# Attention with routed experts on one core: the products with V two key tiles at a time, behind every second block of scores

## The chip, the core and the metric

The kernel runs on one core of a Trainium2 chip. The engines of that core run side by side, each through its own queue in order: TensorE (PE; its weight loads are listed apart as PEld), VectorE (DVE), ScalarE (ACT), GpSimd (POOL) and SyncE (SP), which here issues nearly all transfers. They wait for each other by semaphores. The metric is the time of one execution in microseconds (us) on the device.

## The reference

Three stages, one behind the other. The change lies in the first.

```python
def _attn_ref(q, k, v, centroids):          # q, k, v: 2 x 8 x 768 x 64
    ...
    q_assign = np.argmax(np.einsum('bhsd,hcd->bhsc', q_n, c_n), axis=-1)
    k_assign = np.argmax(np.einsum('bhsd,hcd->bhsc', k_n, c_n), axis=-1)
    mask = q_assign[:, :, :, None] == k_assign[:, :, None, :]
    scores = scale * np.matmul(q, k.transpose(0, 1, 3, 2))
    scores = np.where(mask, scores, -1000000000.0)
    scores = scores - np.max(scores, axis=-1, keepdims=True)
    attn = np.exp(scores)
    attn = attn / (np.sum(attn, axis=-1, keepdims=True) + 1e-09)
    return np.matmul(attn, v)
```

Behind it every token goes to one of 8 experts (two products with a ReLU between, weighted by the gate's probability), and a last stage multiplies a projection of the tokens with the sigmoid of a causal convolution over them and projects once more.

## The kernel before

The attention goes through 8 groups `g`, each one batch and two heads (768 queries, 768 keys, 64 dimensions). A group has two units `u` of 384 queries, 16 units in all. A unit has 6 blocks `j`: three query tiles `t` of 128 rows by two heads `h`. The main loop (L748) runs over the 96 blocks `i`; "block 8" below means `i % 12 == 8`, that is a place in the group, unless a unit is named.

What one block issues, in this order:

- `do_S(i + 2)`: the scores of the block after next, 128 queries by 768 keys, in a PSUM tile `s` (pool `ps_s`, two slots). Two products of L607 and two of L611, the latter with 80 rows that hold the rest of the split and the mask. VectorE takes the row maximum `mx` (L618).
- `do_T(i)`: six transposes of the probabilities `pexp` (L642), three for each half of the keys, into PSUM tiles `tp` of 3 x 128 columns (pool `ps_t`, two slots, so one for each half). A copy carries each half to `pt` in SBUF: the second half by ScalarE (L647), the first by VectorE (L645) in blocks 0, 1, 7, 8, 10 and 11, and by ScalarE in the others and all through the last unit.
- `do_exp(i + 2)`: ScalarE's exponential with the row sum (L627), from `s` to `pexp`.
- `do_PV(u - 1, j)`: for key tile `j` of the unit before, the products of V with the transposed probabilities (L654): two, one for each head. The stationary tile is 128 keys x 64 dimensions, so head 0 fills the rows 0 to 63 of `pv` in PSUM and head 1 the rows 64 to 127; the six key tiles of a unit are summed there. `pv` has one slot. Behind key tile 5 ScalarE copies it to `ut` (`post1`, L663).
- The preparation of the next group, one list per block: in block 0 the products `dott` (L349, a stationary tile 32 wide) and ScalarE's L331, in block 1 `dots` (L359) and L334, in blocks 2 and 4 the choice of the cluster on VectorE (and GpSimd), in block 5 the transposes `pr` (L388) and ScalarE's `ohr` (L398), and SyncE's transfers of the stacked operands `st` in blocks 3 and 5.
- `post2(u - 2)`: in block 3 of a unit (in groups 4 and 5 in block 4 of a unit) the products `po` (L679), which turn `ut` back to rows of tokens and form the router's logits.

In the last unit (`u == 15`) the products with V of unit 14 are issued three key tiles at a time in its first two blocks, and its own go query tile by query tile (`last_PV`). In the first unit there are none. In groups 4 and 5 the blocks 6 to 9 also carry the routing of the first batch, small operations on VectorE for the most part.

A schedule written out by hand sets the order on every engine: each engine runs its instructions as the code issues them. `tc.manual_schedule()` leaves that order alone and adds the waits. A product that writes to a PSUM slot waits until the copy that read the slot before is through.

Of the kernel before, what the change touches and what calls it, by code (L numbers as in the profile page):

```python
# [16 lines left out]
DRAM = bass.MemoryType.DRAM  # L17
# [15 lines left out]
def routed_attention_moe_kernel(  # L33
# [65 lines left out]
    nc.scalar.activation(warm[:, 1:2], warm[:, 0:1], AF.Sqrt)  # L99

    def keep_warm(ps, n):
        """Products that nothing reads, so that the array's clock is up when the data arrive."""
        for _ in range(n):
            nc.tensor.matmul(ps, onesb, onesb.unsqueeze(1).to_broadcast([128, 4, 128]), start=True, stop=True)

# [38 lines left out]
    nc.scalar.dma_start(cw64, convw.bitcast(I32).rearrange("p (f w) -> p f w", w=2))  # L144

    def fill_slots():
        """Every place of a row starts as zeros that belong to no token; one piece per call."""
        padrow = wstg.tile([128, XC], F32, tag="w", name="padrow")
        nc.gpsimd.memset(padrow, 0.0)
        nc.gpsimd.memset(padrow[:, 513:514], PADID)  # L150
        for d, n in ((xslots, E * CAP // 128), (xover, NCH)):
            dv = d.rearrange("(r p) c -> p r c", p=128)
            for r in range(0, n, 2):
                yield nc.sync.dma_start(
                    dv[:, r:r + 2], padrow.rearrange("p (o c) -> p o c", o=1).to_broadcast([128, 2, XC])
                )
# [2 lines left out]
    cs = cst.tile([128, 6, 4], F32, name="cs")  # L159

    def cent_norm():
        """One over each centroid's norm: the square root once more by Newton's step."""
        v = nc.vector
        v.tensor_tensor(csq, cent_sb, cent_sb, op=ALU.mult)
        v.tensor_reduce(cs[:, 0], csq, axis=AX.X, op=ALU.add)
        nc.scalar.activation(cs[:, 1], cs[:, 0], AF.Sqrt)
        v.tensor_scalar(cs[:, 1], cs[:, 1], 1e-30, None, op0=ALU.max)
        v.reciprocal(cs[:, 2], cs[:, 1])
        v.tensor_tensor(cs[:, 2], cs[:, 2], cs[:, 0], op=ALU.mult)
        v.tensor_tensor(cs[:, 3], cs[:, 1], cs[:, 2], op=ALU.add)  # L170
        v.tensor_scalar(cs[:, 4], cs[:, 3], 0.5, 1e-6, op0=ALU.mult, op1=ALU.add)
        v.reciprocal(cs[:, 5], cs[:, 4])
# [8 lines left out]
    nc.vector.memset(cumb[:, 0, :], 0.0)  # L181
    nc.vector.tensor_copy(xnat[:, :, 513], tokid)

# [1 line left out]
    worder = []  # L185
    for e in range(E + 1):
        worder += [(e, 0), (e, 1)]
# [5 lines left out]
    wld = dram.tile([2, 128, 2048], F32, name="wld")  # L193

    def double_bits(w, t1, t2, top):
        """Of doubles w: the 29 last bits t1, sign and exponent t2, and the float32 just below in size, top."""
        lo, hi = w[:, :, 0], w[:, :, 1]
        v = nc.vector
        return [
            lambda: v.tensor_scalar(t1, hi, 3, 0x3FFFFFF8, op0=ALU.logical_shift_left, op1=ALU.bitwise_and),  # L200
            lambda: v.scalar_tensor_tensor(t1, hi, -0x40000000, t1, op0=ALU.bitwise_and, op1=ALU.bitwise_or),
            lambda: v.scalar_tensor_tensor(t1, lo, 29, t1, op0=ALU.logical_shift_right, op1=ALU.bitwise_or),
            lambda: v.tensor_scalar(t2, hi, 0x7FF00000, None, op0=ALU.bitwise_and),
            lambda: v.scalar_tensor_tensor(
                top, t2, float(897 << 20), t1.bitcast(F32), op0=ALU.is_ge, op1=ALU.mult
            ),
            lambda: v.tensor_scalar(t1, lo, 0x1FFFFFFF, None, op0=ALU.bitwise_and),
            lambda: v.tensor_scalar(t2, top.bitcast(I32), -0x00800000, None, op0=ALU.bitwise_and),
        ]

    def convert_steps(ws):
        """The output stage's doubles, as a rounded float32 and its rest, to DRAM: one entry per step."""
        steps = []
        wi = ws.rearrange("p a b -> p (a b)")
        raw = [wi[:, 1024 * r:1024 * r + 1024] for r in range(2)]
# [61 lines left out]
    ovf = {}  # L277

    def raw(j):
        """The overflow's first weights stay whole: float32 products suit its few columns better."""  # L280
        return worder[j] in ((E, 0), (E, 1))

    def w_dma(j):
# [34 lines left out]
        nc.scalar.copy(hi[:, c], t[:, c])  # L318
        (lo_eng or nc.vector).tensor_tensor(lo[:, c], t[:, c], hi[:, c].bitcast(F32), op=ALU.subtract)  # L319

# [1 line left out]
    def prep_steps(g):  # L322
        b, p = pairs[g]
        x = X[g]
# [86 lines left out]
            nc.sync.dma_start(st[h][64:80, 3, :].bitcast(F32), r[16 * h:16 * h + 16, :])  # L411

        def S0(h, parts=None):
            """The first scores, from the parts where they lie; the mask when it is there."""
            if parts:
                S_[h] = ps_s.tile([128, 2, 512], F32, tag="s", name="s")
                r = slice(64 * h, 64 * h + 64)
# [156 lines left out]
    scattered = {}  # L574

    def scatter(dst, idx, src, n, why=None):
        """Rows to dst at idx, those at n or beyond left out; no two rows of a dst share a place."""
        ins = nc.gpsimd.indirect_dma_start(
            out=dst[:, :],
            out_offset=bass.IndirectOffsetOnAxis(ap=idx, axis=0),  # L580
# [112 lines left out]
    last = {}  # L693

    def last_PV(t):
        """The last unit goes tile by tile, so that little of it is left behind the last scores."""
        g = items[6 * UL][0]
        if t == 0:
            PVs[UL] = ps_v.tile([128, 384], F32, tag="pv", name="pv")
# [48 lines left out]
    for i in range(NI):  # L748
# [9 lines left out]
        if u == U - 1:  # L758
# [2 lines left out]
                    do_PV(u - 1, 3 * j + kt)  # L761
            if j == 1:
                post1(u - 1)
        elif u:
            do_PV(u - 1, j)
            if j == 5:
                post1(u - 1)
        if i % 12 < len(prep):
# [45 lines left out]

    keep_warm(ps_t.tile([128, 512], F32, tag="t", name="spin3"), 34)

# [1 line left out]
    tot = small.tile([128, E], F32, tag="tot", name="tot")  # L818
    nc.vector.tensor_copy(tot, carry["tot"])
    cmp_ = small.tile([128, E, NCH], F32, tag="cmp", name="cmp")  # L820
# [27 lines left out]
    nc.vector.tensor_copy(idx1, osl)  # L848
    aps.close()

# [1 line left out]
    xs_p = mpool("xs", 2)  # L852
    xt_p = mpool("xt", 2)
    h_p = mpool("hp", 2)
# [157 lines left out]

    keep_warm(ps_h.tile([128, 512], F32, tag="h", name="spin"), 20)

# [1 line left out]
    nch = nc.values_load(infoi[0:1, 0:1], min_val=0, max_val=NCH)  # L1016
    with tc.For_i(1, nch, 1) as j:
        ej = nc.sync.value_load(infoi[0:1, bass.ds(j + 1, 1)], min_val=0, max_val=E - 1)
        if True:
# [29 lines left out]
            y = y_p.tile([128, 512], F32, tag="y", name="yl")  # L1049
            nc.scalar.activation(y, yp, AF.Copy, scale=xs[:, 0, 512:513])  # L1050
            scatter(x2d, ids[:, 0:1], y, 2 * S)
# [1 line left out]
    mps.close()  # L1053
    moe.close()
    fin = ExitStack()
# [189 lines left out]
```

## Time and profile before

| | |
|---|---|
| median of 3 runs | 593.78 us (593.48 to 594.0) |
| span of the profiled execution | 598.3 us |
| TensorE busy | 566.0 us, 95% |
| weight loads (PEld) | 438.5 us, 73% |
| VectorE | 391.5 us, 65% |
| ScalarE | 334.5 us, 56% |
| GpSimd | 156.0 us, 26% |

A line of a timeline gives the start from the span's start, the length, the engine, the source line and the operation with the tiles that it writes and reads; "x2" merges equal instructions in a row, and a bracket gives the idle time of that engine before and what ended it. The ends of TensorE's products are modelled and overlap the next start, so the distance between two starts is the measure there. A float32 product appears as two records, so the two products of one key tile with V are "x4". The attention takes the span up to some 275 us, the experts up to some 480, the last stage the rest.

### The profile page before, as it was taken

The page shows a single profiled execution, that of the slowest core. Times are in us where ns is not written, and L with a number is a line of the kernel's source. Part 1 is how long each engine was busy: PE and PEld are TensorE (multiplying, and loading weights), DVE is VectorE, ACT ScalarE, POOL GpSimd, SP SyncE. Part 2 cuts the span into 40 slices and gives each one's busy share as a digit, 9 for nine tenths or more (in the row PEclk, how much of TensorE's full clock was granted, in tenths as well). Part 3 has the DMA queues.
Part 4 walks back from the last instruction along what each step waited for, and adds up shares of the span by engine and source line. Part 5 has one row for each costly group of instructions (what it writes and reads, how often), then busy time and mean ns, then how long its engine had stood idle before and what let it go on. Part 6 is the DMA issues. An engine that isn't in the chain of part 4 may idle for free. (4 is left out here: it accounts for less than half of the span.)

```text
span 598.3 us, 9364 instructions
## 1 busy us (share of the span) xinstructions
PE 566.0 (95%) x3474; PEld 438.5 (73%) x3474; DVE 391.5 (65%) x644; ACT 334.5 (56%) x603; POOL 156.0 (26%) x121
## 2 busy tenths in 40 slices
PE   8599999999999999997889999999999998887997
PEld 3376666666766666674689989989889884776886
DVE  6375666566787875557358688687677480799940
ACT  3387767686767677763146555637555352363432
POOL 3101010010121110113450504406235333555320
PEclk8699999999999999998889999999999998998999
DMA  6967776664564737021637688685786865600112
GB/s 146 258 136 231 163 230 148 210 129 124 113 192 83 204 78 210 1 72 65 244 115 272 220 286 275 218 295 200 264 309 222 356 260 203 263 1 1 54 72 88
DMA packets 33103, 104.82 MB, mean 175 GB/s; under 512 B 5713, under 2 KB 6225, under 8 KB 27936
## 3 DMA queue, kind: packets, MB, share of 16 engines
q1 hardware_dynamic: 29104, 97.84, 53.0%
q0 software_dynamic: 3280, 6.32, 2.8%
q8 instruction: 28, 0.46, 0.3%
q10 hardware_dynamic: 672, 0.06, 0.1%
q14 instruction: 19, 0.16, 0.1%
HBM read 63.45 MB, written 24.95 MB: 148 GB/s over the span
## 5 line engine op out<-in xcount | busy, mean ns | idle before, releaser
L618 DVE TENSOR_REDUCE mx<-s 128x1 f32<-128x768 f32 x96 | 91.7, 956 | 66.9 <-PE s L611 62.7
L319 DVE TENSOR_TENSOR wlo<-wraw,whi 128x1024 fp32r<-128x1024 f32 x66 | 85.5, 1297 | 33.9 <-ACT whi L318 33.3
L647 ACT COPY pt<-tp 128x384 f32<-128x384 f32 x148 | 65.8, 482 | 68.9 <-PE tp L642 66.6
L318 ACT CAST whi<-wraw 128x1024 fp32r<-128x1024 f32 x68 | 70.1, 1044 | 42.5 <-DMA wraw<-in_wq_dram 39.5
L627 ACT ACTIVATE pexp<-s,mx 128x768 f32<-128x768 f32 x96 | 87.0, 906 | 3.1 <-DVE mx L618 2.6
L642 PE MATMUL tp<-ident,pexp 128*128 128x128 f32 x576 | 79.6, 274 | 0.0
L654 PE MATMUL pv<-pt,vt 128*64 128x384 f32 x360 | 77.1, 510 | 0.0
L642 PEld LDWEIGHTS tp<-ident,pexp 128*128 128x128 f32 x576 | 69.2, 141 | 4.2 <-ACT pt L647 0.5
L607 PE MATMUL s<-st 128*128 128x384 f32 x188 | 58.1, 390 | 1.7 <-ACT pexp L627 1.7
L607 PEld LDWEIGHTS s<-st 128*128 128x128 f32 x188 | 28.5, 190 | 37.1 <-ACT pt L647 22.7
L976 PE MATMUL yp<-whi,hhi 128*128 128x512 f32 x136 | 53.8, 396 | 0.0
L979 PE MATMUL yp<-wlo,hhi 128*128 128x512 f32 x136 | 53.7, 395 | 0.0
L980 PE MATMUL yp<-whi,hlo 128*128 128x512 f32 x136 | 53.7, 395 | 0.0
L1113 DVE SCALAR_TENSOR_TENSOR gt<-xf,convw_sb,gt 128x768 f32<-128x768 f32 x32 | 52.2, 1648 | 1.7 <-ACT gt L1109 1.1
L611 PE MATMUL s<-st 80*128 80x384 f32 x188 | 49.0, 342 | 0.0
L337 POOL TENSOR_TENSOR xx<-xkq,xx 128x768 fp32r<-128x768 f32 x8 | 14.5, 1815 | 123.9 <-DVE dsb L354 71.7
L236 POOL TENSOR_TENSOR wspace<-wspace 128x512 f32<-128x512 f32 x8 | 14.3, 1784 | 117.8 <-ACT wspace L232 106.8
L949 PE MATMUL hps<-xhi,whi 128*128 128x256 f32 x256 | 42.9, 288 | 1.4 <-ACT xhi L923 0.7
L953 ACT ACTIVATE hhi<-hps 128x512 fp32r<-128x512 f32 (+1 forms) x36 | 20.7, 575 | 41.1 <-PE hps L949 32.9
L949 PE MATMUL hps<-xhi,wlo 128*128 128x256 f32 x256 | 42.1, 287 | 1.0 <-issue 1.0
L949 PE MATMUL hps<-xlo,whi 128*128 128x256 f32 x256 | 41.4, 284 | 0.0
L954 DVE SCALAR_TENSOR_TENSOR hlo<-hps,hhi 128x512 fp32r<-128x512 f32 (+1 forms) x36 | 23.7, 658 | 24.0 <-issue 15.7
(218 smaller groups left out, 983.1 us busy)
## 6 DMA issues: line engine op xcount, KB each, us to landing
wraw<-in_wq_dram SPq DMA_DIRECT2D x34, 1024.0 KB, 5.5
st<-xx SPq DMA_DIRECT2D x48, 384.0 KB, 6.9
xkq<-in_kq_dram SPq DMA_DIRECT2D x16, 384.0 KB, 4.4
xslots<-padrow SPq DMA_DIRECT2D x8, 514.0 KB, 7.8
wspace<-in_wd_dram SPq DMA_DIRECT2D x8, 512.0 KB, 5.4
xs<-xslots SPq DMA_DIRECT2D x7, 514.0 KB
vt<-in_v_dram SPq DMA_DIRECT2D x8, 384.0 KB, 4.9
out_dram<-os SPq DMA_DIRECT2D x11, 256.0 KB, 2.0
```

Source lines behind the costliest of these rows:

```text
L318: nc.scalar.copy(hi[:, c], t[:, c])
L319: (lo_eng or nc.vector).tensor_tensor(lo[:, c], t[:, c], hi[:, c].bitcast(F32), op=ALU.subtract)
L607: nc.tensor.matmul(ps[:, n, :384], st[:, 1, q0:q0 + 128], st[:, 0, 384 * n:384 * n + 384], start=True, stop=False)
L618: nc.vector.tensor_reduce(mx, ps[:, :, :384], axis=AX.XY, op=ALU.max, negate=True)
L627: nc.scalar.activation(pt, ps[:, :, :384], AF.Exp, bias=mx[:, 0:1], accum_out=Zt[i // 6][:, t, h:h + 1])
L642: nc.tensor.transpose(tp[:, k, :], p[:, 128 * kt:128 * kt + 128], ident)
L647: nc.scalar.copy(dst, tp)
L654: nc.tensor.matmul(PVs[u][64 * h:64 * h + 64, :], Vt[g][:, kt, h, :], PT[u, h][:, kt, :], start=(kt == 0), stop=(kt == NQT - 1), skip_grou ...
L949: nc.tensor.matmul(hp[:, fi, :w], a[:, d, fs], c[:, d, :w], start=(n + d == 0), stop=(n + d == 5))
L976: nc.tensor.matmul(yp[t], hhi[:, fa, ts], whv[:, f, :], start=(q == 0 and f == 0), stop=False)
L979: nc.tensor.matmul(yp[t], hhi[:, fa, ts], wlv[:, f, :], start=False, stop=False)
L980: nc.tensor.matmul(yp[t], hlo[:, fa, ts], whv[:, f, :], start=False, stop=(q == 1 and f == 3))
```

## The change

In units 1 to 14 an even block issues no product with V any more, and an odd one issues those of two key tiles, its own and that of the block before: j = 0 and 1 behind block 1 of the unit, 2 and 3 behind block 3, 4 and 5 behind block 5. The first and the last unit stay as they are. The diff also drops comments and docstrings, which changes no instruction.

```diff
--- before.py
+++ after.py
@@ -761,8 +761,9 @@
                     do_PV(u - 1, 3 * j + kt)
             if j == 1:
                 post1(u - 1)
-        elif u:
-            do_PV(u - 1, j)
+        elif u and j % 2:
+            for kt in (j - 1, j):
+                do_PV(u - 1, kt)
             if j == 5:
                 post1(u - 1)
         if i % 12 < len(prep):
```

TensorE in unit 1, blocks 6 and 7 of group 0, before (`s` scores, `tp` transposes, `pv` products with V; pt_316 and pt_348 are the two heads' transposed probabilities of unit 0):

```order
L607 MATMUL s<-st_192 128x384 x2
L611 MATMUL s<-st_192 128x384 x2
L642 MATMUL tp<-ident,pexp 128x128 x6
L654 MATMUL pv<-pt_316,vt 64x384
L654 MATMUL pv<-pt_348,vt 64x384
L607 MATMUL s<-st_193 128x384 x2
L611 MATMUL s<-st_193 128x384 x2
L642 MATMUL tp<-ident,pexp 128x128 x6
L654 MATMUL pv<-pt_316,vt 64x384
L654 MATMUL pv<-pt_348,vt 64x384
```

The same place after:

```order
L607 MATMUL s<-st_192 128x384 x2
L611 MATMUL s<-st_192 128x384 x2
L642 MATMUL tp<-ident,pexp 128x128 x6
L607 MATMUL s<-st_193 128x384 x2
L611 MATMUL s<-st_193 128x384 x2
L642 MATMUL tp<-ident,pexp 128x128 x6
L654 MATMUL pv<-pt_316,vt 64x384
L654 MATMUL pv<-pt_348,vt 64x384
L654 MATMUL pv<-pt_316,vt 64x384
L654 MATMUL pv<-pt_348,vt 64x384
```

The transposes of the even block are followed at once by the next scores, and four products with V stand together.

TensorE in block 9 of group 0 with its waits, after (Activation_49 is ScalarE's semaphore, DVE_49 VectorE's; the block before, 8, is one in which VectorE copies the first half):

```order
L607 MATMUL s<-st_308 128x384 [waits Activation_49]
L607 MATMUL s<-st_308 128x384
L611 MATMUL s<-st_308 128x384 x2
L642 MATMUL tp<-ident,pexp 128x128 [waits Activation_49]
L642 MATMUL tp<-ident,pexp 128x128 x2
L642 MATMUL tp<-ident,pexp 128x128 [waits DVE_49]
L642 MATMUL tp<-ident,pexp 128x128 x2
```

The waits are those of before. The first three transposes wait for ScalarE, the other three for VectorE: the first half of block 9 has been given the slot that the second half of block 8 had, and the other way round. Where ScalarE copied both halves, both wait for ScalarE, and each half has the slot of the same half before. On VectorE, ScalarE, GpSimd and SyncE the order of the instructions stays as it was.

TensorE in block 0 of group 1 after, where the products with V of the even block stood ahead of `dott`:

```order
L642 MATMUL tp<-ident,pexp 128x128 x6
L349 MATMUL dott<-xkq,cd 32x384 x4
L607 MATMUL s<-st_308 128x384 x2
L611 MATMUL s<-st_308 128x384 x2
L642 MATMUL tp<-ident,pexp 128x128 x6
L654 MATMUL pv<-pt_481,vt 64x384
L654 MATMUL pv<-pt_501,vt 64x384
L654 MATMUL pv<-pt_481,vt 64x384
L654 MATMUL pv<-pt_501,vt 64x384
L359 MATMUL dots<-ident,dsb 128x128 x3
```

`dott` now follows the transposes, and `dots` four products with V.

## Rows read from the trace of the kernel before

**Rows 1.** Busy time by stretches, one stretch: PE, PEld, DVE, ACT, POOL (counts), PEclk, DMA, GB/s.

```profile
100.00:150.00 50.00, 50.00 (x316) 33.61 (x314) 30.30 (x49) 35.83 (x76) 2.82 (x2) 1.00 0.61 159
```

**Rows 2.** Timeline, one block in the middle: start us, length us, engine, line, operation [idle before].

```profile
71.25 0.62 PE L607 MATMUL s<-st 128*128 128x384 f32 x2
...
72.07 0.82 PE L642 MATMUL tp<-ident,pexp 128*128 128x128 f32 x6
...
72.34 0.96 DVE L618 TENSOR_REDUCE mx<-s 128x1 f32<-128x768 f32 x1 [1.40 <-PE s L611]
...
72.82 0.87 PE L654 MATMUL pv<-pt,vt 128*64 128x384 f32 x4
...
72.92 0.48 ACT L647 COPY pt<-tp 128x384 f32<-128x384 f32 x1 [0.75 <-PE tp L642]
...
73.21 0.55 DVE L645 COPY pt<-tp 128x384 f32<-128x384 f32 x1
...
73.61 0.62 PE L607 MATMUL s<-st 128*128 128x384 f32 x2
```

**Rows 3.** Timeline, the last unit's three V tiles in a row, PE and one weight load.

```profile
261.58 2.16 PE L654 MATMUL pv<-pt,vt 128*64 128x384 f32 x12
...
261.96 0.14 PEld L654 LDWEIGHTS pv<-pt,vt 128*64 128x64 f32 x2 [0.18 <-issue]
...
263.67 0.62 PE L607 MATMUL s<-st 128*128 128x384 f32 x2
```

**Rows 4.** Timeline, the first unit, which has no products with V.

```profile
31.65 0.82 PE L642 MATMUL tp<-ident,pexp 128*128 128x128 f32 x6
...
32.23 0.60 PE L607 MATMUL s<-st 128*128 128x384 f32 x2
...
32.61 0.86 ACT L647 COPY pt<-tp 128x384 f32<-128x384 f32 x2
...
32.66 0.52 PE L611 MATMUL s<-st 80*128 80x384 f32 x2
...
33.14 0.70 PEld L642 LDWEIGHTS tp<-ident,pexp 128*128 128x128 f32 x6 [0.28 <-ACT pt L647]
...
33.14 0.93 PE L642 MATMUL tp<-ident,pexp 128*128 128x128 f32 x6
...
34.41 0.62 PE L607 MATMUL s<-st 128*128 128x384 f32 x2 [0.34 <-ACT pexp L627]
```

**Rows 5.** Timeline, block 0 of a group: V products, then dott.

```profile
54.19 0.87 PE L654 MATMUL pv<-pt,vt 128*64 128x384 f32 x4
...
54.99 0.85 PE L349 MATMUL dott<-xkq,cd 128*32 128x384 f32 x8
```

**Rows 6.** Timeline, a block in which ScalarE copies both halves.

```profile
61.58 0.82 PE L642 MATMUL tp<-ident,pexp 128*128 128x128 f32 x6
...
62.10 0.86 ACT L647 COPY pt<-tp 128x384 f32<-128x384 f32 x2 [0.57 <-PE tp L642]
```

**Rows 7.** Timeline of ScalarE from block 5 into block 6.

```profile
68.30 0.92 ACT L627 ACTIVATE pexp<-s,mx 128x768 f32<-128x768 f32 x1
...
69.19 0.49 ACT L663 COPY ut<-pv 128x384 f32<-128x384 f32 x1
...
69.54 1.00 ACT L398 ACTIVATE ohr<-pr,rowb 64x768 fp32r<-64x768 bf16 x1
...
70.43 0.85 ACT L647 COPY pt<-tp 128x384 f32<-128x384 f32 x2
```

**Rows 8.** Timeline, block 6 of the first group: scores, and ScalarE's copies.

```profile
38.26 0.62 PE L607 MATMUL s<-st 128*128 128x384 f32 x2
...
40.49 0.84 ACT L647 COPY pt<-tp 128x384 f32<-128x384 f32 x2
```

**Rows 9.** Timeline, the last unit: transposes, then the products of L679.

```profile
264.48 0.82 PE L642 MATMUL tp<-ident,pexp 128*128 128x128 f32 x6
...
265.14 0.91 PE L679 MATMUL po<-wgl_sb,ut 128*128 128x146 f32 x6
```

## The prediction

> **What bounds the kernel now.** I read the busy time by stretches first: from 100 to 150 us, in the middle of the attention, TensorE is busy for all 50.00 us at a granted clock of 1.00, that is 2.4 GHz, with VectorE at 30.30 and ScalarE at 35.83 [rows 1]. Then the timeline of one block there [rows 2]: TensorE goes from scores (L607, L611) to transposes (L642) to the products with V (L654) to the next scores, and no row of its own has idle time. So what counts there is the distance from one group's start to the next group's start, which holds its stream, its pipeline and whatever the switch costs: scores to transposes 72.07 - 71.25 = 0.82 us, transposes to V 72.82 - 72.07 = 0.75, V to the next scores 73.61 - 72.82 = 0.79. A block is 2.36, two blocks are 4.72. The other engines follow: the maximum starts 1.09 behind the block's start (72.34), the copy of the second half of the transposes 1.67 behind it (72.92, ScalarE), VectorE's copy of the first half 0.87 behind the maximum (73.21), ending 0.55 later, at 2.51. ScalarE had been idle for 0.75 us before its copy.
>
> **The change, and what it removes.** No product is added or taken away. The products with V of an even block move behind those of the odd block that follows. It happens in units 1 to 14 (blocks 6 to 89), three pairs of blocks in each: 42 pairs. Call the even block A and the odd one B. Three prices are needed that a pair of today doesn't show.
>
> First, two key tiles in a row. The last unit already does three in a row: from their start to the next scores 263.67 - 261.58 = 2.09 us [rows 3], where one takes 0.79. So each further tile adds (2.09 - 0.79) / 2 = 0.65, and two take 1.44 where two times one took 1.58: 0.14 saved.
>
> Second, transposes followed at once by scores, which is what A becomes. The first unit has no products with V, and there 32.23 - 31.65 = 0.58 us [rows 4]. Transposes followed by the products of L679 took 265.14 - 264.48 = 0.66 [rows 9]. I take 0.58, since it is the same two instructions, against 0.75 before the V products: 0.17 saved. Bounds 0.09 (by 0.66) and 0.17.
>
> A pair then is 0.82 + 0.58 + 0.82 + 0.75 + 1.44 = 4.41, so 0.31 less than now, as long as TensorE waits for nobody.
>
> The Trainium skill, "TensorE: Matmul & The Clock Gate", section "The mechanism" of the part on packing small matmuls, speaks against the first price: it says that weight loads overlap with running matmuls only where their row groups differ, and here all four products use all 128 rows. By it the loads of the second tile would lie bare; two loads of a head take 0.14 [rows 3], so a tile would add 0.28 more and the pair 4.69. The 2.09 us of three tiles hold their loads already, so this trace does not bear it out.
>
> **What the removed work was covering.** The V products of A stood between the transposes of A and the next scores, and gave ScalarE and VectorE 0.79 + 0.17 us to empty the two PSUM slots of the transposes. That cover goes: from the start of A to the transposes of B it was 2.36 + 0.82 = 3.18, now it is 0.82 + 0.58 + 0.82 = 2.22. The rows of the order show what each half of B's transposes waits for.
>
> Where ScalarE copies both halves (A is block 2, 4 or 6 of twelve): the copies start 62.10 - 61.58 = 0.52 behind the transposes [rows 6], so at 1.34, the first is through after 0.48 at 1.82, the second at 1.34 + 0.86 = 2.20. The first half is wanted at 2.22, the second a half group later, about 2.5. Nothing is late. ScalarE must be free at 1.34: the exponential of the block before starts at about 2.2 of B and lasts 0.9, B is 3.01 long, so it is over at about 0.1 of A. The tightest is block 6, ahead of which ScalarE has ut and ohr: its copies came 70.43 - 68.30 = 2.13 behind the start of the exponential [rows 7]. With the exponential at 2.2 to 2.7 of a B of about 3.3 they come at 1.0 to 1.5 of A, and end their first half by 2.0: still before 2.22.
>
> Where VectorE copies the first half (A is block 0, 8 or 10): here the slots change places, and the first half of B waits for ScalarE's copy (1.67 + 0.48 = 2.15), the second for VectorE's (2.51). A wait was answered 0.05 behind the copy's end in the first unit: the copies begin at 32.61, the first lasts 0.48, and the transposes start at 33.14 [rows 4]. So the first half may go at 2.20 and is wanted at 2.22; the second may go at 2.56 and is wanted at about 2.55. Both are on the edge. In that same row the weight load, too, starts only at 33.14, and the group takes 0.93 instead of 0.82: a start whose load couldn't run ahead costs 0.11. I charge 0.11 for each half: 0.31 - 0.22 = 0.09 a pair. The bounds are no charge (0.31), and B's first half waiting for VectorE after all: 2.56 + 0.11 - 2.22 = 0.45, so -0.14 a pair.
>
> The other kinds. In block 0 of groups 1 to 6 the V products are followed by dott, not by scores. What goes is their 0.80 [rows 5]; dott has a narrow stationary tile as V has, so I let the transposes in front of it keep their 0.75; B gets 0.65: 0.15 saved, and dott itself keeps the transposes of B from being early. In groups 4 and 5 the L679 products stand in blocks 4 and 10: there 0.75 + 0.79 becomes 0.66 [rows 9] and B gets 0.65, so 0.23 saved. The very first pair, blocks 6 and 7 of group 0, has ScalarE late from the first unit: copies at 40.49 - 38.26 = 2.23 [rows 8], first half through at 2.71, so the transposes of B go at 2.76 + 0.11, and the pair is 2.87 + 0.75 + 1.44 = 5.06: 0.34 lost.
>
> **The sum.** 18 pairs by 0.31 = 5.58 (12 in groups 1, 2, 3, 6, 4 in groups 4 and 5, 2 in group 7). 13 pairs with VectorE's copy by 0.09 = 1.17 (2 in group 0, 8 in groups 1, 2, 3, 6, 2 in groups 4 and 5, 1 in group 7). 6 pairs with dott by 0.15 = 0.90, 4 by 0.23 = 0.92, one by -0.34. Together 8.2 us. The routing work on VectorE in groups 4 and 5 has no charge of its own; the bounds below hold it. What stands behind the attention waits for its end, so the 8.2 go through. The profiled execution spans 598.3 us and would span 590.1; the runs' median is 593.78, 4.5 lower, and by the same ratio it goes to **585.6**. With no charge for VectorE's pairs the gain is 8.2 + 13 x 0.22 = 11.1 (582.7); with their -0.14 it is 8.2 - 13 x 0.23 = 5.2 (588.6).
>
> **Rivals.** (1) Slower: ScalarE becomes the one waited for. Place: the copies behind the transposes of A, with 0.96 us less cover. Price: the first pair's -0.34 in each of the 31 pairs that I count at 0.31 or 0.09, so -10.5 + 0.9 + 0.9 - 0.3 = 9.0 lost, 602.8. It decides from the point at which ScalarE's copy of the half that is wanted first ends more than 0.31 - 0.11 = 0.2 behind 2.22. For it: the first unit, where TensorE does wait for an exponential (34.41, 0.34 idle) and for copies (33.14) once the V products are missing [rows 4]. Against it: there every block lacked them; here only every second one does, the mean pair of 4.41 leaves ScalarE two exponentials and at most four copies of some 4.0 us, and before its copies ScalarE was idle for 0.57 and 0.75 [rows 2, 6].
> (2) Bare weight loads: 0.28 for each of 42 second tiles, 11.8 lost against the sum, so 8.2 - 11.8 = 3.6 slower, 597.4. It hangs on what [rows 3] contradict; the page that states it is the one named above.
> (3) The attention gets shorter but the end does not: the expert stage finds its weights or its tokens not there sooner. Time 593.8. For it: weight loads of 1 MB start in the last blocks. Against: the tokens that it starts from are made by the last unit, which the change leaves as it is and moves forward.
>
> **How the numbers follow.** The forecast with its bounds has 0.78, of which about 0.1 lies beyond them on either side still on the faster side; rival 1 0.12, rival 2 0.02, rival 3 0.06, and 0.02 for a gain that all but cancels. A measurement can tell 0.2%, 1.2 us. Faster 0.79, same 0.07, slower 0.14. The range goes from 581.5, a little under the no-charge end since 0.58 rests on one row, to 590.5, where nearly half the sum is lost; slower cases stay outside.
>
> **What would show it.** In the changed profile: from the start of two V tiles to the next scores 1.44 us; transposes to scores 0.58 in A; plain pairs of 4.41; pairs at blocks 8 and 10 between 4.41 and 4.86, with a wait of the transposes of B for pt copies where I am right about the edge; the last unit some 8 us earlier, and everything behind it by as much. Wrong would be: waits of TensorE for pt copies or exponentials in blocks 3, 5 and 7; a second V tile of more than 0.65; an attention that ends 8 us earlier with the same end of the kernel.

## The result, and the profile after

The changed kernel takes 585.1 us (median, 583.75 to 586.31) where the kernel before takes 593.63 (592.52 to 594.0): a ratio of 0.984, with an interval of 0.982 to 0.987. A second measurement of the same kernel gave 585.03, ratio 0.985 (0.982 to 0.988). The forecast was 585.6.

The busy time by stretches, in the middle of the attention, answers [rows 1] (columns as there):

```profile
93.00:143.00 50.00, 50.00 (x334) 36.39 (x333) 32.62 (x55) 36.94 (x80) 2.82 (x2) 1.00 0.68 174
```

TensorE is still busy for all 50 us at the full 2.4 GHz, and holds 334 product records where there were 316. The timeline of one plain pair of blocks, TensorE alone, answers [rows 2] (start, length, engine, line, operation):

```profile
98.53 0.62 PE L607 MATMUL s<-st 128*128 128x384 f32 x2
...
99.34 0.82 PE L642 MATMUL tp<-ident,pexp 128*128 128x128 f32 x6
99.92 0.60 PE L607 MATMUL s<-st 128*128 128x384 f32 x2
...
100.71 0.82 PE L642 MATMUL tp<-ident,pexp 128*128 128x128 f32 x6
101.46 1.51 PE L654 MATMUL pv<-pt,vt 128*64 128x384 f32 x8
102.90 0.62 PE L607 MATMUL s<-st 128*128 128x384 f32 x2
```

From start to start: scores 0.81, transposes 0.58, scores 0.79, transposes 0.75, two V tiles 1.44, together 4.37. Two blocks of [rows 2] are 4.72: 0.35 gained.

Where the time went is seen by cutting the span at three starts: the scores of block 6 of group 0 (the first block with the change), the first scores of the last unit, and the first product of the experts. TensorE's timeline of the kernel before, then of the changed one, at the last two cuts:

```profile
255.63 0.62 PE L607 MATMUL s<-st 128*128 128x384 f32 x2
...
292.93 1.08 PE L949 MATMUL hps<-xhi,whi 128*128 128x256 f32 x4 [0.72 <-ACT xhi L923]
```

```profile
246.16 0.62 PE L607 MATMUL s<-st 128*128 128x384 f32 x2
...
284.31 0.99 PE L950 MATMUL hps<-xhi,whi 128*128 128x256 f32 x4 [0.72 <-ACT xhi L924]
```

| us | ahead | the 84 changed blocks | last unit and hand-over to the experts | experts to the end | span |
|---|---|---|---|---|---|
| before | 38.26 | 217.37 | 37.30 | 305.37 | 598.3 |
| before, run again | 38.70 | 217.15 | 37.05 | 302.50 | 595.4 |
| after | 39.31 | 206.85 | 38.15 | 300.29 | 584.6 |
| after, run again | 38.05 | 206.82 | 38.51 | 299.92 | 583.3 |

The change acts in the second column: 10.5 us (10.3 between the second profiles). The third gives 0.9 to 1.5 back. The fourth holds a difference of 2 to 5 us that isn't one of the attention: what the first expert's start costs varies from execution to execution, in one and the same kernel, as experiments 3 and 10 show. So the 84 blocks are compared by their stretch in what follows, and the whole kernels by their medians.

### The profile page after: what moved, and what is told of

Its sections match the earlier page's. It is cut to its first block, busy times and chain, and to the rows that moved or that the text cites. A ratio compares the mean times of both kernels' runs of the same rounds, so it can differ in the third digit from the quotient of the medians.

```text
span 584.6 us, 9359 instructions
## 1 busy us (share of the span) xinstructions
PE 553.5 (95%) x3474; PEld 440.0 (75%) x3474; DVE 394.2 (67%) x644; ACT 333.1 (57%) x603; POOL 146.1 (25%) x121
## 5 line engine op out<-in xcount | busy, mean ns | idle before, releaser
L319 DVE TENSOR_TENSOR wlo<-wraw,whi 128x1024 fp32r<-128x1024 f32 x66 | 90.9, 1379 | 22.1 <-ACT whi L318 21.6
L642 PE MATMUL tp<-ident,pexp 128*128 128x128 f32 x576 | 81.5, 278 | 0.4 <-ACT pt L647 0.3
L654 PE MATMUL pv<-pt,vt 128*64 128x384 f32 x360 | 67.8, 498 | 0.1
L950 PE MATMUL hps<-xhi,whi 128*128 128x256 f32 x256 | 41.5, 283 | 0.7 <-ACT xhi L924 0.7
L950 PE MATMUL hps<-xhi,wlo 128*128 128x256 f32 x256 | 40.5, 279 | 0.0
```

The lines of the kernel that those rows point to most:

```text
L642: nc.tensor.transpose(tp[:, k, :], p[:, 128 * kt:128 * kt + 128], ident)
L654: nc.tensor.matmul(PVs[u][64 * h:64 * h + 64, :], Vt[g][:, kt, h, :], PT[u, h][:, kt, :], start=(kt == 0), stop=(kt == NQT - 1), skip_grou ...
L950: nc.tensor.matmul(hp[:, fi, :w], a[:, d, fs], c[:, d, :w], start=(n + d == 0), stop=(n + d == 5))
```

## The experiments

All edits are to the changed kernel unless it says otherwise.

**1. The kernel before, once more**, to see what of the profiled 598.3 us belongs to the kernel.

> The kernel before, unchanged, for a second trace of it: the profiled execution of before spanned 598.3 us, 4.5 more than the median of its runs, and the changed kernel's spanned 584.6, 0.5 less than its median. From the first scores of unit 1 to those of the last block both should be as in the first trace: 217.4 us from block 6 of group 0 to block 0 of the last unit. Theory 1 (all of the gain is made in units 1 to 14): what lies behind the attention lasts as long in this trace as in that of the changed kernel, 330 us, and the 334.6 of the first trace were that execution's own. Rival (the change also shortens what stands behind): it is 333 or more here too.

Measured: span 595.4, time 597.1; counted from the scores that this expectation counts from, 331.5 us to the end, where the first profile had 334.6 and the changed kernel has 330.2: nearer the theory's 330 than the rival's 333, but not all of it. The attention repeats within 0.2 us, the end doesn't. Three profiles have over 302 us from the experts' first product to the end: both of before, and experiment 3's. In these three, and in no other of the kernels compared here, TensorE stands still inside the first expert, for 1.5, 2.1 and 1.7 us, behind no instruction that the profile names. The line in the waits of TensorE, kernel before (total, times, longest), and one of ScalarE's timeline in the same stretch:

```profile
PE hps L949 <- issue: 1.5, 3, 0.8
```

```profile
303.82 0.60 ACT L953 ACTIVATE hhi<-hps 128x512 fp32r<-128x512 f32 x1 [4.35 <-remote]
```

The expectations of experiments 8 and 10 put these standstills down to weights that come late. The first profile speaks against it: the products that stand still from 304.5 on read the first expert's second quarter of the weights, which ScalarE and VectorE had converted before the first expert product, and which the products from 301.27 on had read already. ScalarE is late there as well: the products that it reads at 303.82 had ended at 300.64. The cause stays open.

The second part is the granted clock. Stretches of 4 us from the first expert product on, in the kernel before and in the changed one (the number behind the counts of POOL is PEclk):

```profile
292.93:296.93 4.00, 4.00 (x19) 3.81 (x20) 1.29 (x2) 0.44 (x1) 3.09 (x4) 0.60 0.99 363
...
304.93:308.93 4.00, 2.65 (x13) 2.44 (x14) 2.00 (x5) 1.49 (x3) 3.20 (x3) 0.80 0.28 70
308.93:312.93 4.00, 3.87 (x27) 3.78 (x27) 3.18 (x5) 3.07 (x4) 0.00 (x0) 0.77 0.90 344
```

```profile
284.31:288.31 4.00, 3.90 (x28) 3.51 (x29) 1.29 (x2) 0.59 (x2) 3.08 (x4) 1.00 1.00 398
```

In the kernel before the clock was partly at its lower level (1.2 GHz) in the first expert's first 4 us, behind a hand-over in which TensorE had been idle, and again around and behind the standstills; in the changed kernel it was at 2.4 GHz there. Clocks of 0.60, 0.80 and 0.77 over 4 us each cost at most 1.6 + 0.8 + 0.9 us; with the 1.5 of standstill that is up to 4.8 of the 5.1 us by which the fourth column differs. The 13.7 us between the two profiled spans therefore overstate the change.

**2. Three key tiles at a time**, to see from where on the missing cover costs more than the grouping saves.

```diff
-        elif u and j % 2:
-            for kt in (j - 1, j):
+        elif u and j % 3 == 2:
+            for kt in (j - 2, j - 1, j):
```

> Three key tiles behind every third block instead of two behind every second. If only the switches between the products counted, a triple would go from 7.08 us to 0.82 + 0.58 + 0.79 + 0.58 + 0.79 + 0.75 + 2.09 = 6.40, 0.68 less; 28 triples give 19 us, 574.6. Theory 1 (the switches, less the waits for copies): the second block without V products finds ScalarE still at the exponential, its copies come some 0.45 later than the transposes, the third transposes wait 0.17 and pay 0.11, where VectorE copies two times 0.11: 0.3 to 0.4 a triple stay, 8.5 to 11 us, so 582.5 to 585, about what two tiles give. Rival (ScalarE becomes the bound as soon as two blocks in a row have no V products): slower than with two tiles by 3 us or more, 588 and up.

Measured: 84 blocks in 207.13, no better than two at a time (206.85), and the 0.3 to 0.4 a group of three that theory 1 had; time 584.82, ratio 0.982 (0.975 to 0.989). With nothing late a group of three blocks would take the 6.40 of the expectation where three of [rows 2] take 7.08: 0.68 gained. The groups at blocks 3 to 5 gained 0.69, those at 9 to 11 0.52 to 0.6 (0.01 in group 0), those at 0 to 2 0.47 (0.03 in group 7), and those at 6 to 8 between 0.09 and -0.22 (-0.56 in group 0). In these last TensorE waits for exponentials, five times by 1.7 us in all, and in groups 4 and 5 for the routing on VectorE, twice by 1.1 in all. One place of the first kind in the timeline of ScalarE and TensorE:

```profile
98.33 0.99 ACT L398 ACTIVATE ohr<-pr,rowb 64x768 fp32r<-64x768 bf16 x1
...
99.22 0.84 ACT L647 COPY pt<-tp 128x384 f32<-128x384 f32 x2
...
99.95 0.91 ACT L627 ACTIVATE pexp<-s,mx 128x768 f32<-128x768 f32 x1
...
101.00 0.62 PE L607 MATMUL s<-st 128*128 128x384 f32 x2 [0.34 <-ACT pexp L627]
```

ScalarE works without a gap from ohr over the copies to the exponential, and the scores wait for its end. That is rival 1, and it has a place: the blocks ahead of which ScalarE has ut and ohr.

**3. Two tiles, with the copies of VectorE moved**, so that in no pair does a half of B's transposes wait for the other engine.

```diff
-        do_T(i, act_only=i % 12 in (2, 3, 4, 5, 6, 9) or u >= U - 1)
+        do_T(i, act_only=i % 2 == 0 or u >= U - 1)
```

> Two tiles as in the change, but ScalarE copies both halves in every even block and VectorE the first half in every odd one (in the last unit ScalarE all, as before). Theory 1 (what the 13 pairs with VectorE's copy in the even block lose, 0.11 each in the changed kernel, is the wait for that copy): these pairs go from 4.48 to 4.37 and the kernel is 1.0 to 1.5 us faster than the changed one, 583.6 to 584.1 against 585.1. Rival A (the 0.11 belongs to the place in the group, not to the copy): no difference, 585.1. Rival B (ScalarE has no room for two more copies in blocks 0, 8 and 10): waits of TensorE for ScalarE's copies in blocks 1, 9, 11, and 587 or more.

Measured: 84 blocks in 205.88, 1.0 less than the changed kernel; time 588.97, ratio 0.989 (0.980 to 0.997). Nine pairs, those at blocks 8 and 10 of groups 1, 2, 3 and 6 and at block 0 of group 7, went from 0.24 to between 0.33 and 0.36, as theory 1 had it. Block 8 of groups 4 and 5 stayed at 0.14, and block 6 of group 3 fell from 0.25 to 0.02. The same pair in the changed kernel (TensorE, its loads, both copying engines) and then here:

```profile
103.72 0.82 PE L642 MATMUL tp<-ident,pexp 128*128 128x128 f32 x6
...
104.29 0.59 PE L607 MATMUL s<-st 128*128 128x384 f32 x2
104.57 0.48 ACT L647 COPY pt<-tp 128x384 f32<-128x384 f32 x1 [1.55 <-PE tp L642]
...
104.86 0.55 DVE L645 COPY pt<-tp 128x384 f32<-128x384 f32 x1
...
105.10 0.67 PEld L642 LDWEIGHTS tp<-ident,pexp 128*128 128x128 f32 x6 [0.18 <-ACT pt L647]
105.10 0.90 PE L642 MATMUL tp<-ident,pexp 128*128 128x128 f32 x6
...
105.94 1.51 PE L654 MATMUL pv<-pt,vt 128*64 128x384 f32 x8
```

```profile
103.31 0.86 ACT L647 COPY pt<-tp 128x384 f32<-128x384 f32 x2 [1.16 <-PE tp L642]
103.36 0.59 PE L607 MATMUL s<-st 128*128 128x384 f32 x2
...
103.98 0.75 PEld L642 LDWEIGHTS tp<-ident,pexp 128*128 128x128 f32 x6
104.15 0.82 PE L642 MATMUL tp<-ident,pexp 128*128 128x128 f32 x6
104.90 1.51 PE L654 MATMUL pv<-pt,vt 128*64 128x384 f32 x8
```

In the changed kernel the load of B's transposes waits for ScalarE's copy until 105.10; the products start 0.81 behind the scores, only 0.02 later than the 0.79 of a plain pair, but the group takes 0.84 to the next start instead of 0.75. With both copies on ScalarE, the first half of B's transposes gets the slot of the first half of A's, which ScalarE starts to empty half a group earlier, at 103.31; the load runs ahead at 103.98 and both surcharges are gone. The time did not show the gain. It is one that rival B named, but not for its reason: in the blocks TensorE waits for ScalarE's copy only once, 0.3 us in the first pair. This profile has the low clock and the standstills in the first expert, its experts take 303.57. Hence experiment 10.

**4. Only the pairs at blocks 2, 4 and 6 of a group**, the others as before.

```diff
+        elif u and not 2 <= i % 12 <= 7:
+            do_PV(u - 1, j)
+            if j == 5:
+                post1(u - 1)
         elif u and j % 2:
```

> Two tiles only in blocks 2 to 7 of a group, 21 pairs; blocks 0, 1 and 8 to 11 issue one tile each as before. Theory 1: each pair keeps its own gain. The trace of the changed kernel has 0.34 for a plain pair, 0.14 for blocks 6 and 7 in groups 4 and 5, and -0.31 for the first pair: 12 x 0.34 + 2 x (0.34 + 0.35 + 0.14) + 2 x 0.34 - 0.31 = 6.1 us, so 587.5, and the 21 pairs left out are worth the other 4 or so. Rival (the gain hangs on the whole row of pairs, since each moves ScalarE's backlog into the next): the pairs of blocks 2 to 7 give 5 or less, and blocks 8 to 11 change as well.

Measured: 84 blocks in 211.01, 6.4 less than before; time 590.63, ratio 0.993 (0.990 to 0.997). The kept pairs at blocks 2 and 4 keep their 0.34 to 0.37, those undone have 0.00. So a pair's gain is its own: it neither borrows from its neighbours nor pushes a wait onto them. The time is 3.1 us over the expected 587.5, though the blocks gained 6.4 where 6.1 were expected; the ten times reach from 588.38 to 594.1.

**5. All six tiles behind the last block of a unit.**

```diff
-        elif u and j % 2:
-            for kt in (j - 1, j):
+        elif u and j == 5:
+            for kt in range(6):
```

> All six key tiles of a unit behind its last block, so five blocks in a row without products with V. Measured from the first scores of unit 1 to those of the last unit (84 blocks; 217.2 us before, 206.9 with two tiles, 207.1 with three). Theory 1 (the copies and exponentials need the cover that the V products gave): ScalarE paces the five blocks, as in the first unit, where blocks took 1.65 to 2.2 us instead of 1.40; a unit is then about 1.4 + 4 x 1.95 + 0.82 + 0.75 + 0.79 + 5 x 0.65 = 14.8 or more against 14.2, and the stretch 218 to 230 us, longer than before although five switches of six are gone. Rival (each switch removed is worth its 0.31 whatever stands around it): 217.2 - 14 x 5 x 0.31 = 195.5 us.

Measured: 84 blocks in 212.33, one time of 590.32: 5.0 us shorter than before, where the expectation had them longer. Still it is 5.5 longer than two tiles at a time. With nothing late six blocks would take 0.82 + 5 x 0.79 + 5 x 0.58 + 0.75 + 0.79 + 5 x 0.65 = 12.46 where six of [rows 2] take 14.16, 1.70 gained in each of 14 units, 23.8 in all. TensorE's waits between 37 and 251 us (total, times, longest):

```profile
PE s L607 <- ACT pexp L627: 2.5, 9, 0.4
PE rps L511 <- DVE sc L503: 1.6, 2, 0.8
PE s L611 <- DMA st<-ohr: 1.3, 1, 1.3
...
```

With 1.8 in three lines more they are 7.2 of the 18.8 us that are missing: exponentials, but also the routing on VectorE (rps) and a load of st, none of which TensorE waits for in the kernel before. The rest lies in starts that are late without idle time, like those of experiment 3, and wasn't added up.

**6. On the kernel before: the V products with a stationary tile 128 wide instead of 64**, to see what the 0.14 is that a second tile doesn't pay. It multiplies each head's probabilities with both heads' V, so it doesn't keep the heads apart.

```diff
-                PVs[u][64 * h:64 * h + 64, :], Vt[g][:, kt, h, :], PT[u, h][:, kt, :],
-                start=(kt == 0), stop=(kt == NQT - 1), skip_group_check=True,
+                PVs[u], Vt[g][:, kt, :, :].rearrange("p h d -> p (h d)"), PT[u, h][:, kt, :],
+                start=(kt == 0 and h == 0), stop=(kt == NQT - 1 and h == 1), skip_group_check=True,
```

> The kernel before, but each product with V takes both heads' columns as one stationary tile of 128 x 128 and writes all rows of its PSUM tile; it no longer keeps the heads apart, so what it computes from there on is not the reference's, and only the distances in the attention are read. Theory 1 (the price is that of changing between a stationary tile of 128 columns and one of 64): transposes to V falls from 0.75 to between 0.58 and 0.66 us, and V to the next scores is the stream of two products, 2 x 0.65 = 1.30, plus 0.05 or less, where it is 0.65 plus 0.14 now. Rival (any switch between kinds of products costs this): 0.75, and 1.44.

Measured: span 624.3, one time of 626.07. TensorE's timeline at two places:

```profile
61.22 0.82 PE L642 MATMUL tp<-ident,pexp 128*128 128x128 f32 x6
61.88 1.46 PE L654 MATMUL pv<-pt,vt 128*128 128x384 f32 x4
62.88 0.80 PE L607 MATMUL s<-st 128*128 128x384 f32 x2
...
63.87 0.82 PE L642 MATMUL tp<-ident,pexp 128*128 128x128 f32 x6
64.52 1.46 PE L654 MATMUL pv<-pt,vt 128*128 128x384 f32 x4
65.82 0.91 PE L679 MATMUL po<-wgl_sb,ut 128*128 128x146 f32 x6
```

```profile
70.58 1.46 PE L654 MATMUL pv<-pt,vt 128*128 128x384 f32 x4
...
71.97 0.52 PE L388 MATMUL pr<-identb,oh 128*64 128x128 bf16 x6
```

Transposes to V are 0.65 or 0.66, where they were 0.75 [rows 2]: 0.10 was the price of going into the narrow tile. V to L679, another 128-wide group, is 1.30, which is twice 0.65 and nothing more; V to a 64-wide group is 1.39. V to the next scores is 1.00 and neither the 1.30 of theory 1 nor the rival's 1.44: the record of the scores starts early there, and from it to the transposes it is 0.99 in place of 0.82. So the start of the scores doesn't tell where V's stream ends, and the sum is better taken from transposes to the next transposes.

That is 2.65 here (61.22 to 63.87). Without the 1.30 of V's own stream 1.35 is left, and a block of the changed kernel that has no products with V takes 0.58 + 0.79 = 1.37: the wide V products pay nothing beyond their stream. In the kernel before a block is 2.36, so 0.99 stands against 0.65 for the stream of one key tile. The 0.34 between them is the price of changing to the narrow stationary tile and back, 0.10 of it in front of V and the rest behind it. A pair saves it once, and the plain pairs gained 0.34 to 0.37. By this sum two blocks take 2 x (1.37 + 0.65) + 0.34 = 4.38, and three take 6.40.

**7. Three tiles, with the copies moved** so that ScalarE copies both halves only in the first block of three (not in block 6).

```diff
-        do_T(i, act_only=i % 12 in (2, 3, 4, 5, 6, 9) or u >= U - 1)
+        do_T(i, act_only=(i % 3 == 0 and i % 12 != 6) or u >= U - 1)
```

with the edit of experiment 2.

> Three tiles behind every third block, and the copies divided to suit: ScalarE copies both halves in the first block of a triple alone, except in block 6 of a group, VectorE the first half in all the others. Theory 1 (what three tiles lost against the switches was ScalarE's lateness in the second and third block of a triple): blocks 6 to 8 of a group take 6.5 us or less instead of 7.0, and the stretch from the first scores of unit 1 to the last unit falls from 207.1 to 202.5 to 204.5 us, 2.5 to 4.5 under that of the changed kernel; the time goes to about 581 to 583. Rival (VectorE is now late instead, since its copy stands behind the next maximum): 206 to 208 us, and no gain over the changed kernel.

Measured: 84 blocks in 210.47; time 588.81, ratio 0.991 (0.989 to 0.993). My theory fell. The rival's reason held, and the blocks took longer than its 206 to 208: VectorE becomes late, and TensorE waits for its copies six times, 2.9 us in all. One place in the timeline:

```profile
95.10 0.95 DVE L618 TENSOR_REDUCE mx<-s 128x1 f32<-128x768 f32 x1
...
95.96 0.55 DVE L645 COPY pt<-tp 128x384 f32<-128x384 f32 x1
...
96.56 0.55 PE L642 MATMUL tp<-ident,pexp 128*128 128x128 f32 x3 [0.52 <-DVE pt L645]
```

The copy stands behind a maximum in VectorE's queue, ahead of which stands xnat (94.63), and the second half of the next transposes waits 0.52 for it.

**8. The changed kernel, once more.**

> The changed kernel again, unchanged, beside the runs of this call. Theory 1: the stretch from the first scores of unit 1 to the last unit is 206.9 us as in its first trace, 10.3 to 10.5 under before, and the ratio of the times lies between 0.982 and 0.987. What stands behind the attention differs from execution to execution by several us in any kernel, by when the second and third quarter of the weights land; if the change itself moved that, the stretch behind would differ by the same amount each time.

Measured: 84 blocks in 206.82, median 585.03. The gains pair by pair add up to 10.55 where the first profile had 10.52.

**9. Three tiles where ScalarE has room, two where it hasn't**: triples in the units of blocks 0 to 5 of a group, pairs in those of 6 to 11, ScalarE's copies at 8 and 10 too.

```diff
-        do_T(i, act_only=i % 12 in (2, 3, 4, 5, 6, 9) or u >= U - 1)
+        do_T(i, act_only=i % 12 in (2, 3, 4, 5, 6, 8, 10) or u >= U - 1)
-        elif u and j % 2:
-            for kt in (j - 1, j):
+        elif u and j % (2 if qb else 3) == (1 if qb else 2):
+            for kt in ((j - 1, j) if qb else (j - 2, j - 1, j)):
```

> Three tiles behind every third block in the first unit of a group (blocks 0 to 5), two behind every second in the second unit (blocks 6 to 11), where ScalarE copies both halves in blocks 6, 8 and 10 and VectorE the first half in 7, 9 and 11. From the traces so far, by group: blocks 0 to 5 gave 1.16 us with three tiles and 0.87 with two, blocks 6 to 11 gave 0.67 with three and 1.0 with two and the copies so divided. Theory 1 (each run of blocks keeps what it gave, since a block with V products lets the copies catch up): 2.2 us a group, and the stretch of 84 blocks is 203.5 to 205 us, 2 to 3.5 under the changed kernel's. Rival (lateness is handed on from unit to unit): 206 us or more.

Measured: 84 blocks in 203.56, as theory 1 had it; time 581.18, ratio 0.979 (0.977 to 0.981), the best of all. The units of two triples gain 1.14 or 1.15 in six groups of seven, those of three pairs about 1.03 where no routing runs. In 35 to 250 us TensorE waits twice in all, 0.3 us each.

**10. Experiment 3's kernel, once more.**

> The kernel with two tiles and ScalarE's copies in the even blocks, once more, since its first time was 588.97 us although its 84 blocks took 205.9, 1.0 less than the changed kernel's. Theory 1 (the first trace had TensorE waiting in the first expert for weights, which any kernel may have): 205.9 again for the blocks, and a time at or below the changed kernel's 585.0 in most of its runs. Rival (its earlier end of the attention itself brings the weights' waits): 587 or more again, with the same waits in the first expert.

Measured: 84 blocks in 205.84, median 584.41, ratio 0.983 (0.981 to 0.985); experts 300.93 in place of experiment 3's 303.57. There was no standstill this time, only the low clock at the start (0.59 in the first 4 us). One kernel thus had medians of 588.97 and 584.41 with the same 84 blocks. Of the 3.8 us between its two profiles 2.6 lie in the experts and 1.0 ahead of the blocks; the kernel before, measured beside them, had medians of 596.18 and 594.22. The 1.0 us that the moved copies gain in the blocks can't be told in the time (584.41 against 585.03).

## Why the prediction was right

The mechanism came out as forecast: fewer changes of kind on a saturated TensorE, less a charge in the pairs with VectorE's copy. That the time came within 0.5 us of the forecast is partly luck, since two errors went against each other: the blocks gained 10.5 us, not 8.2, and about 1 us of it was given back where I had let everything through.

**The three prices held.** Two V tiles take 1.44, transposes followed by scores 0.58, transposes followed by V 0.75, as taken from [rows 2 to 4]. That what they save is one price, that of the change of width, is experiment 6's finding; the prediction only took the distances.

**The terms of the sum**, from the distances between scores two blocks apart, before and after:

| pairs | predicted each, sum | measured each | measured sum |
|---|---|---|---|
| 18 plain | 0.31, 5.58 | 0.34 to 0.37 in 15; 0.25, 0.15, 0.13 at block 6 of groups 3, 4, 5 | 5.75 |
| 13 with VectorE's copy | 0.09, 1.17 | 0.22 to 0.28 in 10; 0.08 (group 0), 0.14 and 0.14 (groups 4, 5) | 2.77 |
| 6 with dott | 0.15, 0.90 | 0.14 to 0.16 | 0.91 |
| 4 with L679 in A | 0.23, 0.92 | 0.34 to 0.36 | 1.39 |
| the first | -0.34 | -0.31 | -0.31 |
| together | 8.2 | | 10.51 |

The mis-sized term is that of VectorE's copies, 1.6 of the 2.3 us. I charged 0.11 for each half of B's transposes; nine of the 13 pairs pay 0.11 for both halves together (experiment 3's two timelines: 0.02 late and 0.09 longer). In the single records of the trace, in all nine, 0.05 to 0.06 of the 0.09 lies behind the first of the six products and 0.03 behind the fourth, which begins the second half. The edge itself was judged rightly: VectorE's copy ends 2.51 behind the block's start, as measured before (105.41 - 102.90), the load of the second half follows it by 0.05, and its product starts at 105.49, 0.11 behind the one ahead of it as in a plain group. A load that has to wait on the edge cost 0.03 to 0.06 here, not 0.11. Block 8 of groups 4 and 5 was put with the wrong kind: small products of the routing (L511) stand there between the transposes of A and the next scores, as dott does, and the gain is dott's 0.14, in experiment 3 too.

The term of L679 was mis-sized by 0.12: L679 to the next scores, which I had left at 0.75, takes 0.65 where transposes and not V stand ahead of L679:

```profile
153.63 0.91 PE L679 MATMUL po<-wgl_sb,ut 128*128 128x146 f32 x6
154.28 0.61 PE L607 MATMUL s<-st 128*128 128x384 f32 x2
```

So behind V a part of the price of the way back to 128 columns is paid only one group later. The plain term was 0.03 to 0.04 short, since scores right behind transposes take 0.79, not 0.82.

**ScalarE's tightest place** was named rightly (block 6, behind ut and ohr) but taken to hold everywhere. With the routing of groups 4 and 5 it does not:

```profile
158.48 0.99 ACT L398 ACTIVATE ohr<-pr,rowb 64x768 fp32r<-64x768 bf16 x1
...
159.37 0.84 ACT L647 COPY pt<-tp 128x384 f32<-128x384 f32 x2
...
159.89 0.92 PE L642 MATMUL tp<-ident,pexp 128*128 128x128 f32 x6
```

The copies begin only behind ohr, and the transposes of B follow 0.52 later in the long form of 0.92: 0.14 gained instead of 0.35. These pairs are the beginning of rival 1, which otherwise didn't come: of TensorE's waits between 35 and 256 us of the changed kernel only these two lie in the 84 blocks, both in group 0 (the others, for exponentials and in L388, come ahead of the first changed block).

```profile
...
PE tp L642 <- ACT pt L647: 0.3, 1, 0.3
...
PE tp L642 <- DVE pt L645: 0.2, 1, 0.2
```

Experiments 2, 5 and 7 show where it, or the same on VectorE, begins to decide: from three tiles on, in blocks with other work on top.

**Rival 2**, bare weight loads, is out. 1.44 for two tiles holds four loads. One pair of loads in the changed kernel's timeline, under the V products that started at 105.94:

```profile
106.31 0.14 PEld L654 LDWEIGHTS pv<-pt,vt 128*64 128x64 f32 x2 [0.18 <-issue]
```

The Trainium skill, "TensorE: Matmul & The Clock Gate", section "The mechanism", says in its list that loads overlap with running products only where the row groups differ; ahead of that it also allows a load into the background weight buffer. Products over all 128 rows agree here with the second sentence and not with the first.

**Rival 3**, a shorter attention with the same end, holds for a tenth. Behind the 84 blocks two small losses stand. One is 0.21 in block 0 of the last unit, whose first V products now wait for ut:

```profile
247.93 0.20 PEld L654 LDWEIGHTS pv<-pt,vt 128*64 128x64 f32 x4 [0.38 <-ACT ut L663]
```

The last pair ends with its V products, and ScalarE empties their PSUM slot into ut only then. The other is the hand-over to the experts. The stretch from the last unit's first scores to the experts' first product is 37.1 to 37.3 in both profiles of before and 38.0 to 38.5 in all of the changed kernels, of which the 0.21 explain part in three only (after, after again and experiment 4; in the others block 0 takes 4.40 as before). The step that got longer lies between the last scatter of tokens and their load; before again, then after:

```profile
284.98 0.98 POOL L578 DMA_INDIRECT xslots<-xnat,idx  x1 [0.30 <-issue]
...
288.12 0.80 SPq L896 DMA_DIRECT2D xs<-xslots  x2
```

```profile
275.49 0.97 POOL L578 DMA_INDIRECT xslots<-xnat,idx  x1 [0.30 <-issue]
...
279.54 0.80 SPq L897 DMA_DIRECT2D xs<-xslots  x2
```

From the scatter's end to the load it is 2.2 to 2.4 us in the two profiles of before and 3.0 to 3.3 in all of the changed kernels. Why isn't settled; no run here separates the scatter's own writes from other transfers in flight.

**From span to time.** I scaled the gain from a profile of 598.3 us to a median of 593.78. These differ by more than the 4.5 us that I named, since a span is 1.7 us shorter than the time of its execution (584.6 and 586.31, 595.4 and 597.1): by 6.2. Up to 4.8 of them are the standstills and the low clock of the first expert in that execution (experiment 1), which most timed runs seem not to have had; the rest wasn't traced. So the median gain is that of blocks and hand-over alone, 10.5 - 1.2 = 9.3 by the tables, against 8.5 between the medians, whose interval of the ratio reaches from 7.8 to 10.8 us. Whether the change alters how often the first expert stands still stays open: it did in both profiles of before, not in experiment 6's, whose kernel is that of before in all but the V products, and in one of nine of changed kernels, too few to tell.

## What to carry to other kernels

Price a regrouping on a saturated TensorE from start-to-start distances of neighbouring groups, not from busy times; the saving here was the price of changing the stationary tile's width and back (0.34 us), paid once for two key tiles instead of twice. What the moved work was covering is the real limit: list which engine empties each PSUM slot and what stands ahead of that copy in its queue, block by block, because a grouping that is free in one block (three tiles in the first half of a group) costs a wait in another. So choose it per place (experiment 9: 581.18 us against 585), and compare kernels by the stretch that was changed where the rest of the span varies by more than the effect.

## What the runs showed of the hardware

Starts whose weight load has to wait cost about 0.1 us a group even when its products are only 0.02 us late: 0.84 from transposes to V instead of 0.75, in nine of the 13 pairs with VectorE's copy, 0.06 of it behind the first such load and 0.03 behind the second.

The price of the narrow tile sits in the change of width: 0.34 for the way in and out, 0.10 of it in front, 0.14 up to the next group's start and the rest behind that; in the kernel before V to another 64-wide group took 0.70 where V to 128-wide scores took 0.79. The Trainium skill, "TensorEngine Tiling (Array Packing)", section "Key Properties", says that a change of the tiling mode drains TensorE. Experiment 6 agrees that the change costs time, and gives the size; that it is a drain, no run shows.

The 64-wide products of a tile's two heads take 0.65 us together, as long as one 128-wide product of the same 384 columns: two of those took 1.30 (experiment 6). They run side by side: in the single records of the changed kernel the products of the two heads start 0.01 us apart (105.94 and 105.94).

The clock behind the hand-over differed between executions, with the same kernel and nearly the same idle time ahead. In the 6 us from 18 to 12 us ahead of the first expert product TensorE was busy for 2.5 us, in before and after alike, and in every profile the clock then fell to 0.50 for a few us and came back while TensorE was busy. In the first 4 us of the experts it fell a second time in three profiles (before 0.60, experiment 3 0.60, experiment 10 0.59) and stayed at 1.00 in all the others, the second profile of before among them; what tells these apart the runs don't show.
